# Top-32 attention and hard-swish MLP: where the left-over query rows of each batch stand in the order of work

## The chip, the cores and the metric

The kernel runs on one core of a Trainium2 chip. The metric is the device time in microseconds of one execution, the median of several. In the profile PE is the matrix engine (PEld its weight loads), DVE the vector engine, ACT the scalar engine, POOL the GpSimd engine and SP the engine that issues the DMAs.

## The reference

Attention over 8 batches, 8 heads, 576 positions and head size 64, in which each query keeps only its 32 largest scores, followed by an MLP with a hard-swish gate over the 4608 rows of the result:

```
scores = scale * q @ k.T                  # 576 x 576 for each batch and head
kth    = 32nd largest of each row
scores = where(scores >= kth, scores, -1e9)
attn   = softmax(scores)                  # exp(scores - max) / (sum + 1e-9)
x      = attn @ v                         # heads joined: 4608 x 512
h      = x @ w_in                         # 4608 x 2048
g      = h * clip(h + 3, 0, 6) / 6
out    = g @ w_out                        # 4608 x 512
```

## The kernel before

**Units of work.** Heads are taken in pairs (`Pair`), four pairs to a batch. The 576 queries of a head are four tiles of 128 rows and 64 left over. A `Duo` is one query tile of two pairs, so of four heads: a normal duo has qt 0 to 3 and treats two rows of 576 scores per pair and partition (`nt` = 2). A left-over duo (qt = J = 4, `rest`) packs the 64 left-over queries of the two heads of a pair into one tile of 128, so it has `nt` = 1. A batch has ten duos: eight normal ones and two left-over ones (one for each half of the heads). There are 80 duos; the list `duos` (L410 to L420) sets their order, and everything else follows from a duo's number m in it.

**Order of the left-over duos before.** In batches 0, 1 and 2 they are the last two of the ten, in batch 7 the third and fourth. In batches 3 to 6 they stand apart: the first half's after qt 0, the second half's after qt 2, so at positions 2 and 7 (counted from 0).

**Slots.** The main loop (L576) gives each duo eight slots. In slot i DVE does one round of the search of the 32 largest: `top` (L249), one MAX8 and, but for the last round, one MATCH_REPLACE8 per row. The other steps of a duo are written into later slots, counted from its own first (dictionary `usual`, L538, and `behind`, L543, for most duos): shift 3 and 7, exp 4 and 8 (ACT), inverse 9 and 13 (DVE), weights 10 and 14 (POOL), flip 12 and 16 (transposing DMAs, SP), join 15 on ACT and 19 on POOL, values 25 (PE), place 26 (ACT). The last two duos have their own table (`soon`, L548). The scores of duo m+1 are computed by PE and copied by ACT in slot 1 of duo m (L589). Each engine takes its instructions in this program order.

**Feed-forward.** When both halves of a query tile are placed, `queue` (L448) puts a block for 128 rows of the MLP at the end of `todo`. Left-over rows need two batches to fill a block (64 rows each): they gather in `xr`, and their block is queued when the second half of the odd batch is placed (L481). So there are 32 normal blocks and 4 left-over ones. A block is cut into 16 pieces: eight with matmuls of h (two pieces and one gate for each 512 columns), then eight with matmuls into `acc`. The gates go to POOL two pieces later. `left` counts the pieces that are queued and not yet issued. How many pieces a slot issues is set here:

```
due += ((left > 0) + (left >= 24) / 8 + (left >= 48) / 8) / (2 if u and u.rest else 1)
piece(int(due))
due -= int(due)
```

So a slot of a normal duo issues one piece if any is queued, nine pieces in eight slots from 24 queued, and a slot of a left-over duo half as many. What is still queued after the last slot is issued at the end (L612).

**Around the batches.** The keys and queries of the next batch are loaded while duos 4 to 7 of a batch run and are transposed in duos 5 to 8; its values are loaded in slot 3 of its own duos 1 and 2 (L601). These positions are counted in duos, whatever kind of duo stands there.

Of the kernel before, what the change touches and what calls it, by code (L numbers as in the profile page):

```python
# [29 lines left out]
def kernel(  # L30
# [11 lines left out]
    B, H, S, D = q.shape  # L42
    DM, FF = moe_w_in.shape
    J = S // P
# [365 lines left out]
    duos = []  # L410
    for b in range(B):
        halves = [pairs[b][0:2], pairs[b][2:4]]
        for qt in range(J):
            duos += [Duo(h, qt) for h in halves]


            if qt == (0 if b == B - 1 else J - 1) and not 2 < b < B - 1:
                duos += [Duo(h, J) for h in halves]
            elif 2 < b < B - 1 and qt % 2 == 0:
                duos.append(Duo(halves[qt // 2], J))  # L420
    assert J == NHP == 4
    per_batch = 2 * J + 2
    ND = len(duos)
# [224 lines left out]
```

## Time and profile before

| | before |
|---|---|
| median of 3 runs (lowest, highest) | 1577.45 us (1576.88, 1578.07) |
| the profiled execution, its own time | 1577.86 us |
| its span in the profile | 1576.1 us |
| mean granted PE clock | 0.962 of full |
| PE busy | 1442.0 us (91%) |
| DVE busy | 1466.6 us (93%) |
| POOL busy | 1142.7 us (73%) |
| ACT busy | 1097.2 us (70%) |
| mean DMA rate | 92 GB/s |

The span runs from the first to the last instruction of the profiled execution; 1.8 us of that execution's own time lie outside it. Busy time of PE contains modelled ends, so a PE shown as full need not be at its limit. Times inside the span are counted from its start. "Idle before" is time in which an engine stood still ahead of an instruction, with the one that released it.

### The profile page before, as it was taken

To read this page: it belongs to the slowest core of one execution; us is meant where nothing else is said; L and a number is where in the kernel's file an instruction comes from. 1 tells how busy PE (TensorE), PEld (TensorE's weight loads), DVE (VectorE), ACT (ScalarE), POOL (GpSimd) and SP (SyncE) were. 2 spreads that over 40 slices of the span, in tenths; PEclk is the share of its full clock that TensorE was granted. 3 is DMA by queue.
4 is the path that set the end of the run, shared out by engine and by line. 5 is a ranking of instruction groups with operands and counts; after the bars stand their busy time and mean duration, and the time that the engine had idled before them with its cause. 6 is when DMAs were issued, how large, how long until landed. Compare 5 with 4: busy or idle time off the path is not lost.

```text
span 1576.1 us, 28787 instructions
## 1 busy us (share of the span) xinstructions
PE 1442.0 (91%) x10272; PEld 1031.7 (65%) x10272; DVE 1466.6 (93%) x3105; ACT 1097.2 (70%) x1865; POOL 1142.7 (73%) x1264
## 2 busy tenths in 40 slices
PE   5355799879999999998999999998999999999899
PEld 3142666567767777676777777776777777776675
DVE  6999999999999999999999999999999999999700
ACT  6675776777877777777776786777776786777521
POOL 4868687777867777867687777867687777867831
PEclk9577899989999999999999999999999999999999
DMA  8552544444444543545254544445254443533410
GB/s 237 158 183 42 116 83 83 89 94 98 73 96 86 101 84 78 99 87 117 54 104 81 98 88 83 94 91 113 58 105 81 98 88 82 103 58 68 83 22 14
DMA packets 450319, 144.49 MB, mean 92 GB/s; under 512 B 433280, under 2 KB 441472, under 8 KB 450176
## 3 DMA queue, kind: packets, MB, share of 16 engines
q1 hardware_dynamic: 450176, 142.65, 43.7%
q8 instruction: 81, 1.33, 0.3%
q14 instruction: 62, 0.51, 0.1%
HBM read 45.09 MB, written 9.44 MB: 35 GB/s over the span
## 4 chain that ended last, share of the span: by engine, by line
DVE 74%; PE 12%; POOL 6%; issue 4%; ACT 2%; SPq 1%; DMA 1%; POOLq 0%
DVE m L256 39%; DVE wk L260 34%; PE acc L391 5%; PE h L371 5%; POOL e L312 1%; PE pv L344 1%; POOL a L109 1%; POOL sc L303 1%; ACT sc L284 1%; POOL w_in L123 1%; DVE den L293 1%; PE big L238 1%; POOL w_out L123 1%; DMA st<-in_moe_w_in_dram 1%; POOL eT L324 1%
## 5 line engine op out<-in xcount | busy, mean ns | idle before, releaser
L256 DVE MAX8 m<-wk 128x8 f32<-128x576 f32 x864 | 613.6, 747 | 2.2
L391 PE MATMUL acc<-w_out,g 128*128 128x512 f32 x1152 | 518.2, 601 | 18.1 <-POOL g L386 18.1
L371 PE MATMUL h<-xT,w_in 128*128 128x128 f32 x4096 | 482.9, 278 | 18.3 <-ACT xT L354 18.3
L371 PEld LDWEIGHTS h<-xT,w_in 128*128 128x128 f32 x4096 | 472.5, 194 | 40.6 <-issue 18.4
L260 DVE MATCH_REPLACE8 wk<-m,wk 128x576 f32<-128x576 f32 x576 | 424.0, 743 | 0.0
L303 POOL TENSOR_SCALAR sc<-sc,den 128x576 f32<-128x576 f32 x288 | 213.2, 750 | 241.2 <-DVE den L293 223.4
L391 PEld LDWEIGHTS acc<-w_out,g 128*128 128x128 f32 x1152 | 213.5, 191 | 265.5 <-issue 238.6
L312 POOL COPY e<-sc 128x2304 uint16<-128x2304 uint16 (+1 forms) x192 | 320.0, 1676 | 10.1
L279 ACT ACTIVATE sc<-sc,m 128x576 f32<-128x576 f32 x288 | 209.8, 774 | 76.3 <-DVE m L256 75.9
L284 ACT ACTIVATE sc<-sc,shift 128x576 f32<-128x576 f32 x288 | 220.2, 767 | 52.1 <-POOL shift L272 50.0
L324 ACT COPY eT<-t 128x2304 uint16<-128x2304 uint16 (+1 forms) x82 | 216.0, 2634 | 44.5 <-DMA t<-e 39.8
L344 PE MATMUL pv<-eT,vm 128*64 128x128 f32 (+1 forms) x2560 | 164.1, 273 | 58.7 <-ACT eT L324 44.0
L260 DVE MATCH_REPLACE8 wk<-m,sc 128x576 f32<-128x576 f32 x288 | 212.0, 743 | 0.0
L344 PEld LDWEIGHTS pv<-eT,vm 128*64 128x64 f32 x2560 | 135.1, 141 | 110.3 <-ACT eT L324 48.2
L324 POOL COPY eT<-t 128x2304 uint16<-128x2304 uint16 (+1 forms) x78 | 203.6, 2610 | 4.5 <-DMA t<-e 4.3
L256 DVE MAX8 m<-sc 128x8 f32<-128x576 f32 x288 | 203.4, 744 | 1.5 <-ACT sc L242 1.5
L386 POOL TENSOR_TENSOR g<-g,hs 128x512 f32<-128x512 f32 x144 | 184.8, 1283 | 12.1
L379 ACT ACTIVATE g<-h,three 128x512 f32<-128x512 f32 x144 | 98.3, 683 | 133.8 <-PE h L371 123.1
L238 PE MATMUL big<-kq 64*128 64x512 f32 x512 | 136.1, 651 | 0.0
L239 ACT COPY sc<-big 128x2048 f32<-128x2048 f32 (+1 forms) x65 | 119.2, 1833 | 17.4 <-PE big L238 17.2
L385 POOL TENSOR_SCALAR g<-g 128x512 f32<-128x512 f32 x144 | 89.0, 618 | 51.9 <-ACT g L379 40.7
L401 ACT ACTIVATE o<-acc 128x512 f32<-128x512 f32 x36 | 21.4, 594 | 89.1 <-PE acc L391 89.1
(47 smaller groups left out, 1087.3 us busy)
## 6 DMA issues: line engine op xcount, KB each, us to landing
landed<-in_k_dram SPq DMA_DIRECT2D x64, 128.0 KB, 2.9
landed<-in_q_dram SPq DMA_DIRECT2D x64, 128.0 KB, 2.9
st<-in_moe_w_in_dram SPq DMA_DIRECT2D x16, 512.0 KB, 5.0
vm<-in_v_dram SPq DMA_DIRECT2D x64, 128.0 KB, 2.3
st<-in_moe_w_out_dram SPq DMA_DIRECT2D x16, 512.0 KB, 6.2
out_dram<-o SPq DMA_DIRECT2D x32, 256.0 KB, 2.4
t<-e SPq DMA_TRANSPOSE x160, 4.6
landed<-in_k_dram SPq DMA_DIRECT2D x32, 32.0 KB, 2.5
```

The costliest lines, as they stand in the source:

```text
L238: nc.tensor.matmul(banks[:, 2 * i + hh, :], pr.qT[d, qs], pr.kT[d, :])
L256: nc.vector.max(self.m[u][:, t, 8 * r : 8 * r + 8], self.cur[t])
L260: nc.vector.match_replace(wk, self.m[u][:, t, 8 * r : 8 * r + 8], self.cur[t], LOWEST)
L279: nc.scalar.activation(row, row, AF.Prelu, bias=m[:, t, TOP_K - 1 : TOP_K], scale=-1.0, alpha=FLAT)
L284: nc.scalar.activation(row, row, AF.Exp, bias=self.less[u][:, t : t + 1], scale=-scale / FLAT, accum_out=self.den[:, u, t : t + 1],)
L303: nc.gpsimd.tensor_scalar(row, row, self.den[:, u, t : t + 1], 1.0, ALU.mult, ALU.mult)
L312: nc.gpsimd.tensor_copy(halves[:, :, to : to + c1 - c0], words)
L324: copy(eT[:, 0 : self.nb, :] .rearrange("p c q -> p (c q)") .bitcast(U16) .rearrange("p (x h) -> p h x", h=2), self.t16[u][:, 0 : 2 * self ...
L344: nc.tensor.matmul(pv[hh * D : (hh + 1) * D, u * w : (u + 1) * w], pr.vm[:, hh, c, :] if c < J else pr.vr[:, hh, :], rhs, start=(c == 0), ...
L371: nc.tensor.matmul(h[:, (f - f0) * P : (f - f0 + 1) * P], w_in[:, i, f * P : (f + 1) * P], xT[:, i, :], start=(i == 0), stop=(i == NHP - 1),)
L386: nc.gpsimd.tensor_tensor(g[:], g[:], hs[:], ALU.mult)
L391: nc.tensor.matmul(acc[:], gs[f // nf][:, f % nf * P : (f % nf + 1) * P], w_out[:, f, :], start=(f == 0), stop=(f == NFC - 1),)
```

## The change

Only the list of duos changes. In an even batch both left-over duos come last, in an odd one both come first, so that the four left-over duos of two batches stand in a row. Positions change in batches 1 and 3 to 7; batches 0 and 2 keep theirs. Which slot a step stands in, the piece rule, the loads and the buffers are as before.

```
         halves = [pairs[b][0:2], pairs[b][2:4]]
-        for qt in range(J):
+        for qt in [J, *range(J)] if b % 2 else range(J + 1):
             duos += [Duo(h, qt) for h in halves]
-            if qt == (0 if b == B - 1 else J - 1) and not 2 < b < B - 1:
-                duos += [Duo(h, J) for h in halves]
-            elif 2 < b < B - 1 and qt % 2 == 0:
-                duos.append(Duo(halves[qt // 2], J))
```

## The prediction

> **What bounds the kernel now.** I read the busy table and the slices first.
>
> ```profile
> PE 1442.0 (91%) x10272; PEld 1031.7 (65%) x10272; DVE 1466.6 (93%) x3105; ACT 1097.2 (70%) x1865; POOL 1142.7 (73%) x1264
> ...
> PE   5355799879999999998999999998999999999899
> ...
> DVE  6999999999999999999999999999999999999700
> ```
>
> DVE is full up to slice 38 and then has nothing to do, while PE is busy to the end. So the time is DVE's run plus a tail of PE. In DVE's timeline, from one duo's first maximum to the next one's, a normal duo takes 19.40 us and a left-over duo 11.22 us wherever it stands: no wait shows between duos from 144 us on. The last maximum ends at 1488.3 us. The tail is read in PE's timeline (start, us, instruction; x counts matmuls and weight loads):
>
> ```profile
> 1495.06 4.90 PE L371 MATMUL h<-xT,w_in 128*128 128x128 f32 x32
> 1499.80 10.47 PE L391 MATMUL acc<-w_out,g 128*128 128x512 f32 x24
> ...
> 1512.53 3.70 PE L391 MATMUL acc<-w_out,g 128*128 128x512 f32 x8
> 1516.07 14.45 PE L371 MATMUL h<-xT,w_in 128*128 128x128 f32 x128
> 1530.36 13.90 PE L391 MATMUL acc<-w_out,g 128*128 128x512 f32 x32
> 1544.09 14.46 PE L371 MATMUL h<-xT,w_in 128*128 128x128 f32 x128
> 1558.38 13.90 PE L391 MATMUL acc<-w_out,g 128*128 128x512 f32 x32
> ```
>
> A block is 64 matmuls of h and 16 of acc with their loads: 1544.09 − 1516.07 = 28.0 us, 1.75 us a piece. After DVE's end 8 + 2 + 16 + 16 = 42 pieces follow. Only the last block's 16 had to come so late (the values of the last duo feed it); 26 pieces are debt. Where the debt arose, the table of windows shows (window, its length, busy of PE, PEld, DVE, ACT, POOL; PE clock, DMA share, GB/s):
>
> ```profile
> 300.00:320.00 20.00, 12.05 (x107) 7.46 (x106) 20.00 (x45) 14.47 (x20) 11.22 (x12) 0.91 0.35 73
> 320.00:340.00 20.00, 13.16 (x104) 13.16 (x105) 20.00 (x44) 13.08 (x22) 13.19 (x14) 0.75 0.47 90
> ...
> 360.00:380.00 20.00, 19.49 (x169) 16.67 (x168) 20.00 (x44) 14.79 (x27) 12.99 (x14) 1.00 0.48 102
> ...
> 720.00:740.00 20.00, 14.89 (x110) 12.40 (x111) 19.66 (x42) 14.83 (x28) 14.01 (x15) 0.83 0.56 116
> ...
> 1080.00:1100.00 20.00, 15.65 (x137) 13.77 (x137) 19.66 (x41) 15.72 (x27) 15.47 (x18) 0.91 0.59 117
> ```
>
> PE falls idle around 300 to 340, 730 and 1085 us while DVE runs on: the piece queue is empty there.
>
> **The change: what it moves.** It adds and removes no instruction. DVE's sum (64 × 19.40 and 16 × 11.22) stays. What moves is when blocks are queued, and I count that by the code's own rule: a block adds 16 pieces in the slot of its place; a normal duo issues 8, a left-over one 4; a slot with none queued issues none.
>
> Before: 15 pieces are queued after duo 10 and 7 after duo 11. They are gone after slot 6 of duo 12, and the next block comes in slot 2 of duo 14 (duo 11 + 26 slots): 11 slots without a piece, 11 × 2.43 = 27 us, the first two windows. Further gaps: duo 36 slot 5 to duo 37 slot 1 (windows at 700 to 740) and duo 56 slot 7 to duo 57 slot 1 (at 1085). The extra rate from 24 queued pieces gives one piece more in duos 30, 40, 44, 60, 64 and 76: the six pieces that these later gaps cost. After duo 79: 26 queued, plus the last block, 42. The trace's tail agrees, which checks the count.
>
> After: duos 8 to 11 are all left-over and issue 16 pieces instead of 24, and the left-over block of batches 0 and 1 is queued in slot 2 of duo 14 instead of duo 22. Queued after duo 11: 15; after 12: 7; the last goes in slot 6 of duo 13, and the next block comes in slot 2 of 14. The gap is 3 slots instead of 11: **8 pieces gained**. From there blocks arrive every 16 pieces' worth of slots, through each row of four as well (4 × 4 pieces, one left-over block): after duos 15, 17, ... 77 two pieces are queued, never a slot without one, never 24. After duo 79: 18, plus 16 makes 34.
>
> So 42 − 34 = 8 pieces leave the tail. In its order they are 2 of h (3.6 us) and 6 of acc (10.3 us): **13.9 us**.
>
> **The tail's start.** PE's second half of duo 78's values begins at 1492.73, released by POOL's join of eT. In the new count the gates around it stand four slots earlier. The row of POOL's work there (gate 1.96 us, join 2.8, weights 3.65): two gates now come before the weights of duo 79, which ran at 1484.3, and that chain slips by 1.1; one gate of 1.95 behind them falls away. The join comes 0.85 earlier. I take −0.8, with ends −2 and +2 for the order of these gates. Then eight pieces and the last values follow as before.
>
> **Four left-over duos in a row: does DVE stall?** In 11.22 us instead of 19.40 the other engines must still do what lags from the normal duos. Before, the tightest place is duo 28, the first of two left-over duos. POOL, then ACT:
>
> ```profile
> 584.27 0.61 POOL L385 TENSOR_SCALAR g<-g 128x512 f32<-128x512 f32 x1
> ...
> 593.16 0.61 POOL L385 TENSOR_SCALAR g<-g 128x512 f32<-128x512 f32 x1
> ...
> 595.37 0.22 POOL L272 TENSOR_SCALAR shift<-shift 128x1 f32<-128x1 f32 x1
> ```
>
> The shift of duo 28 was ready at 588.35 (its last maximum) and done at 595.6: POOL was 7.2 us late. ACT waited for it, copied the scores of duo 30 by 598.9, and DVE started that duo at 599.56: 0.67 us to spare, no stall. So 7.2 us is about what DVE tolerates. POOL in duo 28 did 7.3 us of weights, a join of 2.8, three gates (5.9) and small ones.
>
> After, duo 28 issues two acc pieces and two of h, and gates come two pieces later, so it has no gate: lateness 7.2 − 5.9 = 1.3. Duo 29: shifts and memset 1.1, weights of a left-over duo 2 × 2.4, join 2.8, two gates 3.9: 12.6 against 11.2, +1.4. Duo 30: join now 1.9, so 11.7, +0.5. Duo 31: no gate, 7.6, −3.6. Peak 3 to 4 us. In the row of duos 8 to 11 the gates fall in the first two, as before the change (5.7 and 2.9 us to spare there), and the last two have none. PE: duo 28 has 7.0 of pieces, 2.3 values, 1.3 scores, 1.1 transposes, 11.7; then 10.6, 10.6, 11.2: half a microsecond late. ACT: 13.6 in duo 28 (normal exp 3.5, own 2.0, copies 1.3, join 2.8, h copies 1.9, the rest placing and transposes), then 9.6. SP: loading values in slot 3 of duo 31 takes 5 us of issue (1352.8 to 1357.5 for the same step inside left-over duo 72 before) ahead of duo 30's transposing DMA; ACT's join may wait some 3 to 5 us, but the next duo is normal and its reciprocal is due only 14 us later. Stall: 0 taken; bounds 0 and 2 us for each of four rows.
>
> **A rule against the change.** After it, every block starts in the slot in which its input is placed, so PE can run dry 32 times. The Trainium skill, "TensorE: Matmul & The Clock Gate", section "HAM oscillation", asks for no PE gaps over about 3.4 us, since PE then drops to half clock. The windows at 300 to 340 agree (0.91, 0.75). By the rule, a gap at each block with 3.4 us at half clock behind it would cost 1.7 us × 32 = 54 us of PE. But duos 15 to 18 before have exactly this state (2 and 10 queued), and there the wait for the placed input was 0.51 us (at 367.88) with clock 1.00 in the window. I take nothing. PE needs 18.7 us in a normal duo (14.0 + values 2.3 + scores 2.4) of DVE's 19.4, so a wait of half a microsecond is absorbed.
>
> **Sum.** Against the profiled span: 1576.1 − 13.9 − 0.8 = 1561.4; its own time 1577.86 becomes 1563.2, and the median, 0.4 lower, 1562.8.
>
> **Rivals.**
> (1) *Small stalls in the rows*, 1 to 2 us in each of four, 4 to 8 us on DVE's run and so on the end: 1567 to 1571. For it: only 0.67 us to spare before. Against: the gates leave the first duo. 14%.
> (2) *Slower: POOL's lateness adds up.* If the second left-over duo makes POOL as late again as the first did (7.2 us) and the third and fourth do not recover, DVE waits some 7 us in each row, 4 × 7.2 = 29 us, less 14: 1592. It decides from 3.5 us a row. For it: duo 29 still joins a normal duo. Against: its weights shrink from 3.65 to 2.4 each. 7%.
> (3) *Given back*: PE waits for its input at each block and arrives late at the tail by what was saved: 1577, within 0.2%. For it: waits of up to 9.3 us for placed inputs, at 326.84. Against: that wait is the empty queue itself, and PE arrives at the tail ahead, waiting 2.4 and 4.5 us for POOL. 4%.
> The forecast has 75%; its own range is 1560 to 1566. The range 1559 to 1570 takes in most of (1). Faster by over 0.2% (3.2 us, about what a measurement can tell from no change): 75 + 14 = 89%; within 4%; slower 7%.
>
> **What would show it.** Right: DVE's last maximum still near 1488; 34 pieces after it; windows around 300 to 340 nearly full and no dips at 730 and 1085; POOL's shift never over 5 us late in duos 28 to 31. Wrong: DVE waits for the scores or den in left-over rows, or PE's clock under 1.00 after 350 us.

## The result, and the profile after

The changed kernel takes 1568.57 us in the median (1567.61 to 1569.18, 6 runs) against 1577.40 before in the same comparison: a ratio of 0.9943, 95% interval 0.9931 to 0.9956. It is faster, by 8.8 us; 14.7 were forecast. Its profiled execution took 1569.13 us, with a span of 1567.3.

The busy table and the slices of the changed kernel:

```profile
PE 1446.8 (92%) x10272; PEld 1033.0 (66%) x10272; DVE 1466.7 (94%) x3105; ACT 1097.0 (70%) x1865; POOL 1143.8 (73%) x1264
...
PE   5356898899999999999999999999999999999899
...
DVE  6999999999999998999999999999999999999910
...
PEclk9977799999999999999999999999999999999999
```

DVE does the same work (1466.7 us against 1466.6), but slice 16 of its row now shows an 8, and its end moves back. Its last maximum ends at 1495.8 us, 7.5 later than before. What follows is 71.5 us instead of 87.8.

The idle stretches of PE in the table of windows (columns as before the change: length, busy of PE, PEld, DVE, ACT, POOL; PE clock, DMA share, GB/s):

```profile
300.00:320.00 20.00, 15.71 (x116) 11.71 (x115) 20.00 (x45) 10.55 (x16) 11.65 (x13) 0.91 0.50 102
320.00:340.00 20.00, 20.00 (x153) 15.32 (x152) 20.00 (x45) 16.82 (x31) 17.17 (x18) 1.00 0.48 91
720.00:740.00 20.00, 20.00 (x139) 14.13 (x138) 20.00 (x45) 17.27 (x33) 16.97 (x18) 1.00 0.52 89
1080.00:1100.00 20.00, 20.00 (x111) 11.62 (x109) 20.00 (x44) 15.75 (x28) 16.80 (x19) 1.00 0.45 89
```

They are filled but for the short gap that the count leaves at duo 14. PE's timeline at the end:

```profile
1501.22 3.70 PE L391 MATMUL acc<-w_out,g 128*128 128x512 f32 x8
1504.76 10.88 PE L371 MATMUL h<-xT,w_in 128*128 128x128 f32 x96
...
1517.91 3.84 PE L371 MATMUL h<-xT,w_in 128*128 128x128 f32 x32
1521.58 13.90 PE L391 MATMUL acc<-w_out,g 128*128 128x512 f32 x32
1535.32 14.45 PE L371 MATMUL h<-xT,w_in 128*128 128x128 f32 x128
1549.61 13.90 PE L391 MATMUL acc<-w_out,g 128*128 128x512 f32 x32
```

Eight pieces (2 of acc and 6 of h), the last values (at 1515.57, left out), then 2 of h, 8 of acc and a block of 16: 34 pieces, as counted.

**Where the rest went.** DVE's timeline has waits that it did not have before, all of a reciprocal for ACT's den. The largest stands in duo 29, the second left-over duo of batch 2:

```profile
596.62 0.75 DVE L260 MATCH_REPLACE8 wk<-m,wk 128x576 f32<-128x576 f32 x1
601.21 0.16 DVE L293 RECIPROCAL den<-den 128x1 f32<-128x1 f32 x1 [3.83 <-ACT den L289]
```

A second one, of 1.43 us, is in duo 49. A third, of 2.17 in duo 79, costs nothing, since PE reaches the last values without waiting for them. They start at 1515.57 against 1510.19 before: 5.4 later, which is 3.83 + 1.43 and 0.1. With the forecast's 13.9 us for the eight pieces the span would be 1576.1 + 5.4 − 13.9 = 1567.6, against 1567.3 measured. The gain came; 5.3 us of it were given back in two waits.

**The chain behind the wait of duo 29**, in ACT's and then SP's timeline of the changed kernel:

```profile
588.11 0.60 ACT L401 ACTIVATE o<-acc 128x512 f32<-128x512 f32 x1 [3.25 <-PE acc L391]
...
595.32 2.79 ACT L324 COPY eT<-t 128x2304 uint16<-128x2304 uint16 x1 [3.17 <-DMA t<-e]
```

```profile
579.15 2.67 SPq L318 DMA_TRANSPOSE t<-e  x1
588.74 0.36 SPq L403 DMA_DIRECT2D out_dram<-o  x1
589.21 3.54 SPq L318 DMA_TRANSPOSE t<-e  x1
```

ACT stands still for PE's last acc piece before it can copy o. The output DMA needs that copy, and in SP's queue it is ahead of the transposing DMA of duo 27, whose data POOL had ready at 584.3. So that DMA goes out at 589.21, ACT's join waits for it, and the exp of duo 28 behind the join gives its den at 601.2. POOL, which I had feared, was 3.0 us late with duo 28's shift (done 591.63, last maximum 588.59), not 7.2.

PE's piece was late because PE itself was. As its lateness I take how long after a duo's first maximum PE starts the scores for the next one. For duo 27, from DVE's and PE's timelines:

```profile
557.87 1.40 DVE L256 MAX8 m<-sc 128x8 f32<-128x576 f32 x2
564.17 1.09 PE L222 MATMUL big<-kq 64*64 64x512 f32 x8
```

That is 6.30 us in duo 27, 4.44 in duo 47 and 2.80 in duo 67, against −1.3, 0.3 and 0.2 before. The waits behind them are 3.8, 1.4 and 0.

**Why PE is late.** With two pieces queued when a block arrives, the old block ends in slot 1 and the new one starts in slot 2. PE's timeline at duo 22, slots 1 and 2, then ACT's:

```profile
469.85 1.98 PE L391 MATMUL acc<-w_out,g 128*128 128x512 f32 x4
471.67 0.61 PE L371 MATMUL h<-xT,w_in 128*128 128x128 f32 x4
472.78 9.42 PE L371 MATMUL h<-xT,w_in 128*128 128x128 f32 x82 [0.51 <-ACT xT L354]
```

```profile
471.87 0.60 ACT L401 ACTIVATE o<-acc 128x512 f32<-128x512 f32 x1 [2.10 <-PE acc L391]
472.36 0.37 ACT L354 COPY xT<-pv 128x256 f32<-128x256 f32 x1
```

The placing stands behind the copy of o, and that copy waits for PE's last acc piece. So in normal duos PE does not have the input when it asks for it, and waits 0.51 us at block after block: of the 29 blocks that start between 340 and 1480 us, 20 wait for xT (10.4 us in all) and three for the left-over rows in xr; the six without a wait start in a row of left-over duos or in the first duo behind it. From one duo's scores to the next one's, PE takes 19.88 and 18.70 us alternately, 38.6 for two duos of which DVE takes 38.8. In the duos that also transpose the next batch's keys and queries it takes 20.87 and 19.68, so 40.55: there PE falls behind by 1.7 us per pair, and the other pairs give back only 0.2.

### The profile page after: what moved, and what is told of

The parts are those of the page before. It is cut to its first block, busy times and chain, and to the rows that moved or that the text cites. A ratio compares the mean times of both kernels' runs of the same rounds, so it can differ in the third digit from the quotient of the medians.

```text
span 1567.3 us, 28748 instructions
## 1 busy us (share of the span) xinstructions
PE 1446.8 (92%) x10272; PEld 1033.0 (66%) x10272; DVE 1466.7 (94%) x3105; ACT 1097.0 (70%) x1865; POOL 1143.8 (73%) x1264
## 4 chain that ended last, share of the span: by engine, by line
DVE 42%; PE 40%; POOL 6%; ACT 5%; issue 4%; DMA 1%; SPq 1%; POOLq 0%; ACTq 0%
DVE m L256 22%; DVE wk L260 18%; PE h L371 15%; PE acc L391 15%; PE pv L344 5%; PE big L238 3%; POOL e L312 2%; DVE y L118 1%; POOL sc L303 1%; DMA t<-e 1%; ACT eT L324 1%; ACT sc L284 1%; PE big L177 1%; DVE a L117 1%; POOL eT L324 1%
## 5 line engine op out<-in xcount | busy, mean ns | idle before, releaser
L381 ACT COPY hs<-h 128x512 f32<-128x512 f32 x144 | 83.8, 582 | 0.0
```

## The experiments

Each changes one thing in the kernel before or in the changed one, and was timed against the kernel before. First all of them together. "Wait" is PE's usual wait at the start of a block; "late" is PE's lateness, as above, in duos 27, 47 and 67; "DVE" is the sum of DVE's waits from duo 4 to duo 78; then the end of DVE's last maximum and what follows it, in the profiled execution.

```
                       wait   late             DVE   last max   tail   median
before                  -    -1.3  0.3  0.2    0      1488.3    87.8   1577.40
changed                0.51   6.3  4.4  2.8    5.3    1495.8    71.5   1568.57
rows of two            0.51   3.9  6.2  6.2    5.6    1495.8    71.2   1568.83
batch 1 alone          0.51   6.9  0.2  1.6    4.2    1493.5    88.4   1583.65
output DMA on ACT      1.02  12.4 11.0  9.0   15.3    1505.6    70.9   1578.32
values a slot earlier  1.87  17.8 17.8 17.8    50.4   1545.0    68.4   1616.82
output DMA later       0.51   7.2  4.7  3.7    1.4    1491.4    70.9   1565.21
o after the placing    <0.2  -1.0 -1.0 -1.0    0      1490.2    70.9   1563.07
before, values earlier  -     6.2  7.5  8.3    8.4    1497.0    85.7   1585.59
before, o later         -    -1.3  1.5  1.3    0      1487.8    87.1   1577.54
```

**Batch 1 alone: does the filled stretch make the gain?**

```
-        for qt in range(J):
+        for qt in [J, *range(J)] if b == 1 else range(J):
...
-            if qt == (0 if b == B - 1 else J - 1) and not 2 < b < B - 1:
+            if qt == (0 if b == B - 1 else J - 1) and not 2 < b < B - 1 and b != 1:
```

> The kernel before with the left-over duos of batch 1 alone moved to its front. The idle stretch of PE at 300 to 340 us shrinks as in the changed kernel, but by the piece rule the pieces run out later instead (duos 33, 36, 37, 56, 57) and 42 pieces are left for the tail, as before. Count theory: 1575.5 to 1578.5 us. Rival, that the filled early stretch and its clock are the gain: 1562 to 1570.

1583.65 us, ratio 1.0035 (1.0023 to 1.0048): outside both ranges. The count was right: 88.4 us follow DVE's end, 42 pieces and not 34, although this kernel fills 300 to 340 us by the same move as the changed one. So filling that stretch is worth nothing when the pieces run out later; what counts is what is left after duo 79. Most of the slowdown is the other mechanism: in the state with two pieces queued PE comes 6.9 us late to duo 28, and the reciprocal in duo 29 waits 4.24 us, of the 5.8 by which the profiled span is longer.

**Rows of two instead of four.**

```
-        for qt in [J, *range(J)] if b % 2 else range(J + 1):
+        for qt in [0, J, *range(1, J)] if b % 2 else range(J + 1):
```

> The left-over duos last in even batches, but third and fourth in odd ones: rows of two, never four. By the piece rule the tail has 34 pieces as in the changed kernel. Queue theory: a row of two after eight just-in-time duos stalls in its second duo as a row of four does; the waits in duos 29 and 49 stay and the time is 1566 to 1570. Rival, that the row of four is what stalls: no waits, 1562 to 1565.

1568.83 us, ratio 0.9942 (0.9929 to 0.9956), the same as the changed kernel. The waits stand in duos 29, 49 and 69 (1.12, 2.27, 2.17), each the second left-over duo of an even batch. The row of four is not needed for them, and it is not needed for the gain either. Lateness alone does not set the size of a wait: 6.2 us in duo 47 are followed by a wait of 2.27 us here, 6.3 us in duo 27 by one of 3.83 in the changed kernel. From the issue of the transposing DMA to ACT's join 5.0 us pass here and 6.1 there; I did not follow that further.

**Output DMA on ACT's queue.**

```
-                        nc.sync.dma_start(dst, o[p0:p1, :])
+                        nc.scalar.dma_start(dst, o[p0:p1, :])
```

> The changed kernel, with the DMA of the output rows issued from ACT's queue instead of SP's. Queue theory: in duo 28 and 48 the output DMA of the block that ends there stands in SP's queue ahead of the transposing DMA of duo 27 (47) and holds it until PE's late last acc piece is done; ACT's join, its exp and DVE's reciprocal follow late. Then the waits of 3.8 and 1.4 us of the reciprocals in duos 29 and 49 go, and the time is 1562 to 1564.5 us. Rival, that POOL or the compressed row of four itself makes the exp late: the waits stay and the time is 1567 to 1570.

1578.32 us, ratio 1.0004 (0.9996 to 1.0013): no theory expected that. ACT's join in duo 28 indeed no longer waited for its DMA. But the issue now stands on ACT between the copy of o and the placing, where PE waits for it: the wait at most blocks doubles from 0.51 to 1.02 us and PE comes to duo 28 12.4 us late. As a test of SP's queue it is spoilt by that. What it does show is the price: the issue on ACT, with half a microsecond more of waiting at most blocks, costs 10 us.

**Values and placing one slot earlier.**

```
-    behind = dict(usual, values=25, place=26)
+    behind = dict(usual, values=24, place=25)
```

> The changed kernel, with values and place one slot earlier (24 and 25), so that a block's input is placed one slot before its first piece. Queue theory with PE's lateness as its source: the wait of 0.51 us for the placed input at each block goes, PE enters duo 28 less than 3 us late instead of 6.3, the reciprocals wait less than 1 us in all, and by the piece rule one piece less (1.75 us) is left for the tail: 1561 to 1564 us. Rival, that the wait at each block costs PE nothing: only the piece goes, 1566 to 1568.

1616.82 us, ratio 1.0246 (1.0232 to 1.0260). My expectation miscounted: the old block then ends in slot 0, so the new one starts in slot 1, again in the slot of its placing, and there the placing stands behind the copies of the scores. In the list of waits between 340 and 1480 us PE's line reads (us in all, times, longest):

```profile
PE h L371 <- ACT xT L354: 35.6, 19, 1.9
```

With 1.87 us a block PE's two duos take 18.83 + 21.52 = 40.35 us where DVE takes 38.8. PE sets the pace now, and DVE waits 1.3 us or more in every second normal duo from duo 41 to 47 and from duo 61 to 67. This shows how near PE is to the bound. The 48 us are not the longer wait alone, though. Behind 8 of the 19 waits PE's granted clock fell to half for 3.4 us, which shows as 0.91 in the mean of a window of 20 us. One of the eight is the wait before 399.07 (PE's timeline, then the table of windows):

```profile
399.07 8.59 PE L371 MATMUL h<-xT,w_in 128*128 128x128 f32 x60 [1.88 <-ACT xT L354]
400.00:420.00 20.00, 20.00 (x178) 18.97 (x178) 18.30 (x41) 14.30 (x27) 13.30 (x15) 0.91 0.17 33
```

By PE's time from scores to scores, 24.13 us in duo 19 against 22.50 in duo 17, one such stretch costs 1.6 us; eight would be 13 us of PE, which is an estimate.

**The same edit in the kernel before.**

> The kernel before, with values and place one slot earlier, the same edit that made the changed kernel 48 us slower. If that loss needs the just-in-time state (2 or fewer pieces queued when a block arrives), which the kernel before has only in batch 1 and at a few other blocks, the time is 1575 to 1583 us. If values one slot earlier are bad by themselves, it is over 1600.

1585.59 us, ratio 1.0050 (1.0036 to 1.0064), just above the first range and far from the second. The edit costs 48 us in the changed kernel and 8 in this one, so most of the loss needs the state with two pieces queued. What the 8 us are I did not settle: PE is 4 to 11 us late from duo 20 to duo 74 but for duos 37 and 57, and DVE's waits sum to 8.4 us.

**Only the output DMA later.** Its issue is put off by two pieces; the copy of o stays. The new `flush` runs once a piece and issues an entry of `outs` two pieces later; its definition is left out here.

```
-                    for p0, p1, dst in rows:
-                        nc.sync.dma_start(dst, o[p0:p1, :])
+                    outs.append([2, o, rows])
...
+            flush()
```

> The changed kernel, with only the issue of the output DMA put off by two pieces, the copy of o left in its place: PE stays about as late (6 us entering duo 28), but the output DMA no longer stands ahead of duo 27's transposing DMA in SP's queue. If SP's order is the link, ACT's join no longer waits 3.2 and 2.6 us for that DMA in duos 28 and 48, the reciprocals of duos 29 and 49 wait under 1 us each, and the time is 1562 to 1565 us. If ACT is late because its copy of o waits for PE, whatever SP does, over half of the waits stay: 1566 to 1569.

1565.21 us, ratio 0.9920 (0.9906 to 0.9933); 1565 was the end of the first range. SP's, ACT's and DVE's timelines:

```profile
579.42 7.11 SPq L318 DMA_TRANSPOSE t<-e  x2
589.18 0.36 SPq L433 DMA_DIRECT2D out_dram<-o  x1
```

```profile
588.55 0.60 ACT L401 ACTIVATE o<-acc 128x512 f32<-128x512 f32 x1 [3.25 <-PE acc L391]
...
592.35 2.82 ACT L324 COPY eT<-t 128x2304 uint16<-128x2304 uint16 x1
```

```profile
598.26 0.16 DVE L293 RECIPROCAL den<-den 128x1 f32<-128x1 f32 x1 [1.38 <-ACT den L289]
```

The transposing DMA now leaves ahead of the output DMA and ACT's join starts without a wait. PE is later than in the changed kernel (7.2 us), ACT's copy of o still waits 3.25 us for it, and yet DVE's wait falls from 3.83 to 1.38, and the one in duo 49 goes. So SP's order carried 3.9 of the 5.3 us of waits. The remaining 1.4 come through ACT's own wait: from the copy of o to the den of duo 28 its instructions follow one another without a gap.

**The copy of o behind the placing.** The last copy of a block and its output DMA are issued one piece later, in the slot of the next block's first piece, whose placing is issued before.

```
             if f % 2 == 1:
-                if f == NFC - 1:
-                    o = opool.tile([P, DM], F32, tag="o", name="o")
-                    nc.scalar.mul(o[:], acc[:], 1.0 / 6.0)
-                    for p0, p1, dst in rows:
-                        nc.sync.dma_start(dst, o[p0:p1, :])
                 yield None
+        o = opool.tile([P, DM], F32, tag="o", name="o")
+        nc.scalar.mul(o[:], acc[:], 1.0 / 6.0)
+        for p0, p1, dst in rows:
+            nc.sync.dma_start(dst, o[p0:p1, :])
```

> The changed kernel, with the last copy of a block (ACT, o<-acc) and its output DMA issued one piece later, so behind the placing of the next block's input instead of ahead of it. Bubble theory: in the just-in-time state the placing stands in ACT's queue behind the copy of o, which waits for PE's last acc piece, and PE then waits for the placing; that costs PE 1.2 us per block (period of such a duo 19.88 us against 18.70 of its neighbour). With the order turned round the wait of 0.51 us goes, PE enters duo 28 less than 3 us late (6.3 before), the waits of the reciprocals in duos 29 and 49 (3.8 and 1.4 us) go, and the time is 1561 to 1564 us. Rival, that PE's lateness comes from its own work (transposes and pieces) alone: PE stays over 4 us late, the waits stay, 1567 to 1570.

1563.07 us, ratio 0.9909 (0.9895 to 0.9922): the fastest of all. The waits for the placing in its list, for the same stretch:

```profile
PE h L371 <- ACT xT L354: 0.9, 5, 0.3
```

PE's duo with a block's start falls from 19.88 to 19.11 us, it comes to duos 28, 48 and 68 a microsecond early, and no reciprocal waits between duos 4 and 78. The bubble (the time that the wait took from PE) was 0.77 us, not the 1.2 that I wrote into the expectation: the rest of the difference to 18.70 is work, since that duo issues seven pieces of h and one of acc and its neighbour the reverse. This edit cuts two links at once: PE is no longer late, and the output DMA leaves one piece later, in duo 28 behind duo 27's transposing DMA. Against the kernel with only that DMA moved it gains 2.1 us; no run takes PE's wait away and leaves SP's order as it was.

**The same edit in the kernel before.**

> The kernel before, with the copy of o and the output DMA one piece later, as a control of that edit by itself. The kernel before has 10 or more pieces queued at most blocks, so no block waits for its placing, and its tail stays at 42 pieces: 1575.5 to 1578.5 us. Rival, that the later copy helps by itself: 1572 or less.

1577.54 us, ratio 0.9999 (0.9990 to 1.0008). The later copy helps only in the state that the changed order makes: there it is worth 5.5 us.

## Why the prediction came out as it did

The time lies in the stated range, but at the first rival's place (1567 to 1571, given 14%), 2.6 us above the forecast's own range. The forecast's 14.7 us of gain, less 5.3 for DVE's waits and 0.9 for the tail's start, are 8.5; 8.8 were measured.

**The bound and the tail were read rightly.** The count gave the pieces that are left after duo 79: 34 in the changed kernel, 42 in the kernel with batch 1 alone. In duos 30, 50 and 70 the rule does bring the queue to 25 for a slot or two, where the prediction says never 24; the count at the end is the same. The eight pieces came in full: from the last values to the end the changed kernel takes 14.1 us less.

**The tail's start**, put at −0.8 us, came out at +0.1, taken at the last values and less DVE's two waits: in the changed kernel PE waits 4.07 us for POOL's join of duo 77 instead of duo 78's. Where DVE's waits are gone (o after the placing), the last values start at 1509.41, 0.8 before the 1510.19 of before. That has the forecast's size by luck: PE begins the eight pieces ahead of them at 1495.06 in both, and not earlier as forecast; there they are 2 of acc and 6 of h and take 14.35 us, before 2 of h and 6 of acc in 15.13.

**The step that failed is "I take nothing" for the wait at each block, and with it "Stall: 0 taken".** I found the 0.51 us wait in duos 15 to 18 and let it vanish in a slack of 0.7 us a duo. That slack left out the transposes, 1 us in each of four duos a batch, though I had them in the sum for duo 28, and it took 18.70 us for every normal duo, where one in two takes 0.4 more for its seven pieces of h. With both, PE needs 155.4 us for the eight duos 16 to 23 in the kernel where it does not wait (o after the placing), and DVE takes 155.2: over normal duos there was no slack at all. With the wait PE needs 158.3 in the changed kernel, 3 us more than DVE, and the lateness adds up to 6.3 us by duo 27. For duo 28 itself I summed PE's work as if PE began on time: "half a microsecond late".

**The link to DVE was missed, too.** I went through SP's queue in the rows and counted the loads of values, but not the output DMA, which the new count moves ahead of a transposing DMA in just these duos. The first rival had the size (4 to 8 us, 5.3 measured) and the wrong cause: it expected small stalls in all four rows because little time was to spare; there were two, for PE's lateness. That the time fell in the range therefore owes something to the width that the range was given for that rival. With both links cut the kernel takes the 1563 us that the sum gave.

**POOL's lateness adding up (second rival)** did not happen: gates left duo 28 as counted (POOL was 3.0 us late there, where the sum said 1.3), and no wait of DVE stands behind POOL, though its shift is up to 6.6 us late in the first row (duo 9) and 5.2 in the later ones (duo 70). **Given back by PE at the tail (third rival)** did not happen either; PE's lateness reached DVE in the middle instead, and was gone at the end.

**The clock rule.** At 0.51 us a block no half clock followed: from 320 to 1480 us the granted clock of the changed kernel is 1.00 in every window of 20 us but one, which has a wait of 1.86 us, at 670.24, for left-over rows:

```profile
660.00:680.00 20.00, 18.14 (x138) 14.34 (x137) 20.00 (x45) 12.76 (x22) 12.57 (x13) 0.91 0.49 103
```

So the forecast was right to take no half clock at each block, but the rule's 3.4 us is not the limit here: waits of 1.86 and 1.88 us were followed by half clock in this window and behind 8 of the 19 waits of the kernel with values a slot earlier. And a wait that left the clock at 1.00 still cost 0.77 us of PE at block after block.

**The signs named beforehand** came out mixed. For right: 34 pieces, filled windows, and POOL's shift never over 5 us late in duos 28 to 31 (3.0 at most); but the last maximum is at 1495.8, not near 1488. For wrong: both showed, DVE's waits for den in left-over duos 29 and 49, and the clock under 1.00 in the window above.

## What to carry to other kernels

A backlog of work looks like debt at the end of a run, but it is also a cushion: with a queue that is nearly empty each block starts in the slot that makes its input, and a wait that was rare before can be paid at every block. When two engines are within one per cent of each other, sum the second one over a whole period with all that it does, not over the most common step, before calling a wait absorbed. And in a DMA queue that issues in program order, as SP's did here, look at what stands ahead of a transfer: an output that waited for the matrix engine held up a transfer that had been ready for 4.9 us (584.3 to 589.21).

## What the hardware showed unexpectedly

Moving the output DMA from SP's queue to ACT's was no way out: the issue itself is shown with 0.34 us, but standing between two copies on ACT it raised PE's usual wait for the second of them from 0.51 to 1.02 us and made PE 6 us later in duo 27. A wait of 0.51 us on PE with the clock at 1.00 took 0.77 us off its pace; the two matmuls just ahead of it are shown with 0.61 us for the four instructions, where 0.45 would be their share of a block (14.3 us for 128). I did not test what the remaining tenth is. And the granted clock halved for 3.4 us behind some waits of under 2 us, not behind all: 8 of 19 at 1.87 us (values a slot earlier).
